# Two windowed attentions on one core: low parts on VectorE alone, a re-fitted layout clock, earlier release of key buffers, last outputs staged in pbuf

## The chip, the core and the metric

The kernel runs on one core of a Trainium2 chip. TensorE (PE) multiplies matrices, VectorE (DVE), ScalarE (ACT) and GpSimd (POOL) do the elementwise work, SyncE (SP) only issues DMAs. The metric is the device time of one launch in microseconds. Before the change three runs took 1970.92, 1972.98 and 1973.55 us; their median is 1972.98.

## What is computed

Two independent attention layers over 2048 positions with 1024 features and 32 heads of 32 features, all in fp32. Cut to what matters:

```
def A(x, wqkv, wo):               # sliding, dilated: 8 keys, every second position back
    q, k, v = split_heads(x @ wqkv)
    kg, vg = k[:, :, idx], v[:, :, idx]          # idx = pos - 2 * (0..7), masked below 0
    attn = softmax(einsum("bhsd,bhswd->bhsw", q, kg) * 32 ** -0.5)
    return concat_heads(einsum("bhsw,bhswd->bhsd", attn, vg)) @ wo

def B(x, wqkv, wo):               # sliding: the 256 positions up to its own
    q, k, v = split_heads(x @ wqkv)
    p = softmax(where(0 <= i - j < 256, q @ k.T * 32 ** -0.5, -1e9))
    return concat_heads(p @ v) @ wo

out = concatenate([A(...), B(...)], axis=-1)
```

## The kernel before

The work is cut into eight units of 512 positions: four of layer B ("dense" units, 0 to 3) and four of layer A ("window" units, 4 to 7, the even and the odd positions apart, so that the window is 8 neighbours). A unit has eight head groups of four heads. Each fp32 operand is split into a high part of reduced precision and a low part that holds the rest, and every large product is three matmuls: high by high, high by low, low by high (`TERMS`).

Weights and activations come from HBM as 512 KB tiles into three `raw` buffers (`Stream`). `parts` splits them: VectorE casts the high part (L129), and the low part, raw minus high, is made in halves of 512 columns by GpSimd (L134) or by VectorE (L137), whichever the planner expects to be done first, with a bias `POOL_BIAS`. After the first eight tiles GpSimd also issues the loads (L103).

A head group passes these stages. The query and key products (L363, 48 matmuls, t = 0 for queries and 1 for keys) end in a PSUM bank. ScalarE copies the high part out (L314), VectorE makes the low part (L318), and SyncE copies both into the stacked buffers `qst` and `kst` with three DMAs each (L328), after up to three reads of the halo, the keys of the unit before (L308). `qst` and `kst` are double buffered over the head groups, so the copies of head group hg wait for head group hg - 2; they stand in `waiting` until `finish` of that head group. The tiles of `natp`, from which they are copied, are two, so the eighth step of the next head group's product waits for these copies too.

Sixteen first products (L614) give the scores; VectorE finds the row maximum (L619), ScalarE the sum of the exponentials (L624), then its logarithm (L637). VectorE subtracts (L642) and splits the result (L644, L645), one small matmul, the row product (L653), turns it, VectorE copies it out (L657) and SyncE copies it into two further rows of `qst` (L660). The second products (L696 dense, L509 window) then give normalized exponents at once; ScalarE exponentiates them into `pbuf` (L701, L514), and masks are applied by VectorE (L685, L524) or GpSimd (L682, L520). Value products (L741, L548) follow, and `finish` copies their result out as high and low part (L577, L581). After a unit come the output products (L455) with `wo`, which are spread over the next unit's head groups (`O_SLOTS`), as value projections (L415) are over their own (`V_SLOTS`). Outputs go through one staging tile (`stp`, L379 or L382) and are stored by ScalarE's queue (L470).

All of this is put in order when the program is built. There are four lists of items, row products, second and values products, first products, and the large products. The class `Clock` holds the expected free time of each engine and of transfers; the loop at the end of the kernel takes at each step the item that is expected to be ready first. Every engine then runs its instructions in the order in which they were written, so the planner's costs (`C1`, `C3`, `CG`, `CV`, the durations given to `ck.use`, `ck.copy`, `ck.load`, `ck.fetch`) decide the order on every engine but nothing else.

For the last unit the output products of the first `TAIL` outputs run their first seven steps before the last head group is done; the eighth steps follow it.

## Time and profile before

| | before |
|---|---|
| median of three runs | 1972.98 us |
| profiled execution | 1973.82 us |
| its span, first to last instruction | 1972.1 us |
| mean granted TensorE clock | 0.987 |
| DMA | 294.92 MB, 150 GB/s over the span |

How to read it: busy times are per engine. A matmul's own duration overlaps with the next one's, so the rate of the matmuls is read from the chain of work that ended last, which gives stretches of them. "Idle before, releaser" in a group of instructions is the time that the engine stood still ahead of them and what ended it. PEclk is the clock that TensorE was granted; at half clock a matmul takes twice as long while TensorE counts as busy.

### The profile page before, as it was taken

What the parts mean: (1) busy time and instruction counts of PE and PEld (TensorE: products, weight loads), DVE (VectorE), ACT (ScalarE), POOL (GpSimd) and SP (SyncE); (2) the same over time, 40 slices, a digit from 0 to 9 for tenths busy, and PEclk for the clock granted to TensorE, in tenths of its full rate; (3) what the DMA queues carried; (4) which work ended last, traced back from release to release, by engine and by line L of the source; (5) the groups of instructions that cost most, each with busy time, mean ns of one, the idle gap of its engine ahead of it and who ended that gap; (6) DMA issues with size and microseconds to landing.
All of it is one profiled execution on the core that took longest, in us unless ns stands there. A gap on an engine that the chain in (4) does not pass through costs nothing.

```text
span 1972.1 us, 36479 instructions
## 1 busy us (share of the span) xinstructions
PE 1924.7 (98%) x12608; PEld 1619.8 (82%) x12608; DVE 1295.7 (66%) x3762; ACT 957.5 (49%) x3137; POOL 708.7 (36%) x923
## 2 busy tenths in 40 slices
PE   7999999999999999999999999999999999999998
PEld 6878887888877878788878888978888788888886
DVE  5687776678665786567865657655666557666653
ACT  3565554475654656555563344423534334434441
POOL 4334343444433434443443323233332333233221
PEclk9999999999999999999999999999989999999998
DMA  5555546455546465345645647455553565556442
GB/s 176 150 139 153 160 124 178 132 153 157 152 136 174 121 189 149 117 140 148 177 119 146 173 139 196 128 149 170 149 163 116 174 177 162 141 146 172 136 126 75
DMA packets 136502, 294.92 MB, mean 150 GB/s; under 512 B 14464, under 2 KB 42112, under 8 KB 136320
## 3 DMA queue, kind: packets, MB, share of 16 engines
q1 hardware_dynamic: 85632, 124.82, 26.1%
q0 software_dynamic: 40320, 146.82, 22.9%
q10 hardware_dynamic: 10368, 20.98, 2.9%
q8 instruction: 100, 1.64, 0.4%
q14 instruction: 82, 0.67, 0.1%
HBM read 163.58 MB, written 27.26 MB: 97 GB/s over the span
## 4 chain that ended last, share of the span: by engine, by line
PE 84%; DVE 7%; DMA 6%; ACT 2%; issue 1%; SPq 0%; POOL 0%; DVEq 0%; ACTq 0%; POOLq 0%
PE g L363 31%; PE g L455 16%; PE g L415 16%; PE s L614 7%; PE s L696 5%; PE o L741 4%; PE s L509 3%; DMA qst<-rt 3%; PE o L548 2%; DMA kst<-nat 1%; DMA raw<-xs 1%; DVE x L137 1%; DVE w L129 1%; ACT s L624 1%; DVE w L137 1%
## 5 line engine op out<-in xcount | busy, mean ns | idle before, releaser
L363 PE MATMUL g<-x,w 128*128 128x512 f32 x3072 | 801.9, 401 | 8.6 <-DVE w L129 8.0
L134 POOL TENSOR_TENSOR w<-raw,w 128x512 fp32r<-128x512 f32 x225 | 392.5, 1745 | 897.2 <-PE s L614 285.7
L363 PEld LDWEIGHTS g<-x,w 128*128 128x128 f32 x3072 | 562.0, 191 | 110.9 <-DVE w L129 8.4
L624 ACT ACTIVATE s<-s,nm 128x384 f32<-128x384 f32 (+3 forms) x1024 | 452.3, 443 | 231.0 <-DVE nm L619 227.1
L415 PE MATMUL g<-w,x 128*128 128x256 f32 x3072 | 413.3, 285 | 0.0
L415 PEld LDWEIGHTS g<-w,x 128*128 128x128 f32 x3072 | 392.7, 191 | 1.9 <-issue 0.6
L455 PE MATMUL g<-ot,w 128*128 128x512 f32 x1536 | 384.2, 397 | 3.6 <-DVE w L129 2.9
L455 PEld LDWEIGHTS g<-ot,w 128*128 128x128 f32 x1536 | 283.8, 190 | 58.1 <-DVE w L129 3.6
L619 DVE CUSTOM_DVE_ANT_0 s<-s,mask_d 128x384 f32<-128x384 f32 (+2 forms) x512 | 262.0, 556 | 72.9 <-PE s L614 71.5
L614 PE MATMUL s<-kst,qst 96*128 96x384 f32 (+3 forms) x1024 | 238.7, 303 | 16.2 <-ACT s L624 7.1
L701 ACT ACTIVATE pbuf<-s 128x384 f32<-128x384 f32 (+2 forms) x480 | 197.1, 507 | 85.5 <-PE s L696 81.8
L614 PEld LDWEIGHTS s<-kst,qst 96*128 96x128 f32 x1024 | 181.3, 192 | 60.5 <-ACT s L624 18.1
L624 ACT ACTIVATION_READ_ACCUMULATOR s<-s,nm 128x1 f32 x1024 | 210.2, 205 | 0.0
L619 DVE CUSTOM_DVE_ANT_0 s<-s,mask_w 128x136 f32<-128x136 f32 (+1 forms) x512 | 142.4, 322 | 98.4 <-PE s L614 96.8
L129 DVE CAST w<-raw 128x1024 fp32r<-128x1024 f32 x256 | 199.9, 781 | 9.4 <-PE g L455 9.4
L137 DVE TENSOR_TENSOR w<-raw,w 128x512 fp32r<-128x512 f32 x287 | 197.2, 696 | 8.8
L682 POOL TENSOR_SCALAR_AFFINE_SELECT pbuf<-pbuf 128x128 f32<-128x128 f32 (+1 forms) x383 | 147.9, 404 | 150.1 <-ACT pbuf L701 143.5
L314 ACT ACTIVATE nat<-g 128x512 fp32r<-128x512 f32 x128 | 76.6, 598 | 255.2 <-PE g L363 247.8
L318 DVE SCALAR_TENSOR_TENSOR nat<-g,nat 128x512 fp32r<-128x512 f32 x128 | 88.3, 690 | 145.5 <-ACT nat L314 134.9
L524 DVE TENSOR_TENSOR pbuf<-pbuf,keep_w 128x272 f32<-128x272 f32 (+1 forms) x224 | 116.9, 566 | 61.5 <-ACT pbuf L514 60.6
L619 DVE DVE_READ_ACCUMULATOR2_ANT nm<- 128x1 f32 x1024 | 144.3, 141 | 0.0
L696 PEld LDWEIGHTS s<-qst,kst 98*128 98x128 f32 x704 | 106.2, 189 | 37.8 <-PE o L741 10.0
(48 smaller groups left out, 1227.3 us busy)
## 6 DMA issues: line engine op xcount, KB each, us to landing
raw<-wqk POOLq DMA_DIRECT2D x126, 512.0 KB, 3.7
qst<-nat SPq DMA_DIRECT2D x192, 256.0 KB
kst<-nat SPq DMA_DIRECT2D x192, 256.0 KB
raw<-wo POOLq DMA_DIRECT2D x64, 512.0 KB, 3.7
raw<-wv POOLq DMA_DIRECT2D x62, 512.0 KB, 4.5
outs<-ost ACTq DMA_DIRECT2D x64, 256.0 KB
raw<-xs POOLq DMA_DIRECT2D x28, 512.0 KB, 4.8
halo<-nat SPq DMA_DIRECT2D x40, 256.0 KB
```

What stands on the lines that cost most here:

```text
L129: nc.vector.tensor_copy(t[:, 0, :], raw)
L134: nc.gpsimd.tensor_tensor(o, a, b, op=ALU.subtract)
L137: nc.vector.tensor_tensor(o, a, b, op=ALU.subtract)
L363: nc.tensor.matmul(h["ps"], h["w"][:, a, k * P:(k + 1) * P], xt[u][k][:, b, :], start=(k == 0 and i == 0), stop=(k == NK - 1 and i == 2))
L415: nc.tensor.matmul(ps, xt[u][k][:, a, p0:p0 + P], h["w"][:, c, k % kw], start=(k == 0 and i == 0 and r == 0), stop=(k == NK - 1 and i == 2 ...
L455: nc.tensor.matmul(h["ps"], h["w"][:, a, k * P:(k + 1) * P], ot[u, k][:, b, :], start=(k == 0 and i == 0), stop=(k == NK - 1 and i == 2))
L614: nc.tensor.matmul(ps[:, :n], q[0:96, j, b * P:(b + 1) * P], kk[0:96, j, c0:c1], start=True, stop=True)
L619: nc.vector.tensor_tensor_reduce(ps[:, :n], ps[:, :n], mask[:, cut:full], scale=-1.0, scalar=BIG, op0=ALU.add, op1=ALU.min, accum_out=nm)
L624: nc.scalar.activation(ps[:, :n], ps[:, :n], AF.Exp, bias=nm, scale=-1.0, accum_out=sm)
L682: nc.gpsimd.affine_select(w, w, pattern=[[0, m], [step, n]], compare_op=ALU.is_ge, fill=0.0, base=base, channel_multiplier=chan)
L696: nc.tensor.matmul(ps[:, i * n:(i + 1) * n], kk[0:98, j, 256 + kb * P:256 + (kb + 1) * P], q[0:98, j, q0:q0 + n], start=True, stop=True)
L701: nc.scalar.activation(w, ps[:, :pack * n].rearrange("p (j n) -> p j n", j=pack), AF.Exp)
```

## The change

Seven things are done together.

1. `POOL_BIAS` is -99, so every low part of loaded data is made by VectorE. GpSimd keeps masks and the issue of loads. In the masks that may go to either (`keep`) the bias is now `MASK_BIAS`, 0.2 as before, but the times that are compared have changed.
2. `Clock` is rewritten: it knows that some VectorE instructions (`port=True`) and GpSimd exclude each other, it gives every engine its own time from an instruction's end to its being seen, and every kind of transfer its own duration, on one shared list of busy stretches in place of two queues.
3. Costs are re-fitted throughout.
4. The high parts' copies into `qst` and `kst` are planned as soon as ScalarE is done; only the low part's copy follows VectorE. The halo reads move ahead of the query copies.
5. The copies that wait for head group hg - 2 are released 0.3 us after the issue of its last second product (`free_keys`), no longer at `finish`.
6. In the first unit the value projections go to slots 0, 2, 4, 7 (`V0_SLOTS`), no longer 0, 1, 5, 7.
7. In the last unit `TAIL` is 4 (the fourth output takes a PSUM bank of the score ring), outputs are staged in four slots of `pbuf`, and the weights of the last five output products are split as two tiles of 512 columns ("xw"), to be used one by one.

```diff
-POOL_BIAS = 0.6
+POOL_BIAS = -99
+MASK_BIAS = 0.2
+V0_SLOTS = {0:0,2:1,4:2,7:3}
-TAIL, LAND, XAT = 2, 0.45, 1
-C1, C3, CG, CV = 0.114, 0.2, 0.231, 0.243
+TAIL, XAT = 4, 1
+C1, C3, CG, CV = 0.108, 0.2, 0.231, 0.242
...
-    SEM = 0.17
+    SEM = 0.2
+    SEEN = dict(act=0.15, dve=0.115, pool=0.08)
+    LEAD = dict(sp=1.34, act=0.97, pool=1.43)
+    HOLD = dict(sp=0.63, act=0.35, pool=0.6)
+    MOVE = dict(load=(2.12, 0.14), store=(0.64, 0.4), copy=(1.18, 0.56), rows=(0.37, 0.56),
+                halo_out=(0.4, 0.68), halo_in=(0.55, 0.6), halo_few=(0.28, 0.51))
...
+    def start(self, eng, port, *ready):
+
+        t = max((self.free[eng],) + ready)
+        if eng == "pool":
+            t = max(t + 0.06, self.port["dve"])
+        elif port:
+            t = max(t, self.port["pool"])
+        return t
...
-            if max(ck.free["pool"], r) + 1.73 <= max(ck.free["dve"], r) + 0.62 + POOL_BIAS:
+            if ck.ends("pool", 1.15, r) <= ck.ends("dve", 0.61, r, port=True) + POOL_BIAS:
                 nc.gpsimd.tensor_tensor(o, a, b, op=ALU.subtract)
-                end = max(end, ck.use("pool", 1.73, r))
+                end = max(end, ck.use("pool", 1.15, r))
             else:
                 nc.vector.tensor_tensor(o, a, b, op=ALU.subtract)
-                end = max(end, ck.use("dve", 0.62, r))
+                end = max(end, ck.use("dve", 0.61, r, port=True))
...
-            item(p, "w", wo[ly, p[2]])
+            item(p, "w" if p[1] < U - 1 or p[2] < 3 else "xw", wo[ly, p[2]])
...
+            def place(part, e):
+                dst, c = (qst[buf], 0) if t == 0 else (kst[buf], 256)
+                for i, a in enumerate((0, 0, 1) if t == 0 else (0, 1, 0)):
+                    if a == part:
+                        nc.sync.dma_start(dst[i:96:3, :, c:c + S].bitcast(F32), hl[:, a, :].bitcast(F32))
+                        e2 = ck.copy("copy", e, ck.now)
+                return e2
+
+            def stack_hi():
+                if t == 0 and has_halo:
+                    read_halo()
+                h2["hi"] = place(0, r)
+
+            def later(f):
+                if hg < 2 or hg - 2 in done["second"]:
+                    f()
                 else:
-                    waiting.setdefault(hg - 2, []).append(stack)
+                    waiting.setdefault(hg - 2, []).append(f)
...
-                o = stp.tile([P, S], F32, tag="ost", name="ost")
-                e = copy_out(o, h["ps"], h["b"], rg)
+                o = pbuf[:, n % 4, :S] if last else stp.tile([P, S], F32, tag="ost", name="ost")
+                e = copy_out(o, h["ps"], h["b"], ring)
...
+            if ki == nk - 1 and hp == 4 // pack - 1:
+                free_keys(hg)
...
+    def free_keys(hg):
+
+        done["second"][hg] = ck.now
+
+        def go():
+            for f in waiting.pop(hg, []):
+                f()
+
+        ck.defer(ck.now + 0.3, go)
+
     def finish(u, s, h):
         hg = u * NG + s
         done["o"][hg] = ck.now
-        for f in waiting.pop(hg, []):
-            f()
...
         def keep(w, mask, n, m, step, base, chan, r):
-            dur_p, dur_d = m * n / 960 + 0.16, (m * n + 66) / 960
-            if max(ck.free["pool"], r) + dur_p <= max(ck.free["dve"], r) + dur_d + 0.2:
+            dur_p, dur_d = m * n / 960 + 0.13, m * n / 960 + 0.07
+            if ck.ends("pool", dur_p, r) <= ck.ends("dve", dur_d, r, port=True) + MASK_BIAS:
```

## The prediction

> **What bounds the kernel now.** I read the busy times first, then the granted clock, then the stages, then who made TensorE wait.
>
> ```profile
> span 1972.1 us, 36479 instructions
> ...
> PE 1924.7 (98%) x12608; PEld 1619.8 (82%) x12608; DVE 1295.7 (66%) x3762; ACT 957.5 (49%) x3137; POOL 708.7 (36%) x923
> ```
>
> ```profile
> core 0: 1972.1 us, clock 0.987
> ```
>
> TensorE sets the time. It is idle for 1972.1 - 1924.7 = 47.4 us and loses (1 - 0.987) x 1972 = 25.6 us to a halved clock. The change leaves its 12608 matmuls alone, so 73 us is all that any relayout can win. Six stages (start, first unit, its end, the other three dense units, four window units, tail) show where they lie:
>
> ```profile
> core 0: us, PE busy (x) PEld busy (x) DVE busy (x) ACT busy (x) POOL busy (x), PEclk, DMA share, GB/s
> 0.00:40.00 40.00, 29.35 (x152) 24.03 (x153) 22.33 (x48) 11.34 (x20) 17.64 (x28) 0.96 0.66 202
> 40.00:190.00 150.00, 147.97 (x910) 119.01 (x909) 109.35 (x344) 91.75 (x294) 58.42 (x78) 1.00 0.49 139
> 190.00:222.00 32.00, 29.60 (x183) 25.59 (x182) 28.84 (x80) 16.13 (x52) 11.41 (x15) 0.95 0.59 176
> 222.00:1040.00 818.00, 809.13 (x5302) 670.82 (x5302) 569.67 (x1530) 468.92 (x1357) 341.94 (x536) 1.00 0.52 148
> 1040.00:1900.00 860.00, 844.99 (x5710) 728.44 (x5708) 538.01 (x1691) 350.85 (x1357) 269.09 (x257) 0.99 0.55 156
> 1900.00:1972.00 72.00, 63.61 (x363) 51.86 (x361) 27.48 (x73) 18.50 (x60) 10.21 (x11) 0.88 0.19 66
> ```
>
> Idle is 10.7, 2.0, 2.4, 8.9, 15.0 and 8.4 us. The clock is lost in a few places, each row (1 - clock) x 50 us:
>
> ```profile
> 1200.00:1250.00 50.00, 48.20 (x347) 44.00 (x349) 37.34 (x115) 19.32 (x76) 13.80 (x16) 0.93 0.61 174
> ...
> 1450.00:1500.00 50.00, 47.52 (x351) 42.70 (x352) 27.97 (x94) 23.08 (x88) 15.08 (x15) 0.90 0.49 139
> ...
> 1650.00:1700.00 50.00, 47.62 (x334) 41.83 (x334) 39.37 (x122) 22.04 (x88) 14.39 (x15) 0.93 0.65 183
> ...
> 1900.00:1950.00 50.00, 45.08 (x282) 36.84 (x281) 26.10 (x71) 16.15 (x56) 8.43 (x10) 0.83 0.22 75
> ```
>
> That is 3.5, 5.0 and 3.5 us at the ends of three window units and 8.5 us in the tail: 20.5 of the 25.6. The waits of TensorE, by whom it waited for (total, times, longest):
>
> ```profile
> PE g L363 <- DVE w L129: 8.0, 1, 8.0
> PE s L614 <- ACT s L624: 7.1, 8, 1.2
> PE s L509 <- DMA qst<-rt: 6.7, 10, 1.8
> PE s L614 <- DMA kst<-nat: 5.7, 5, 2.0
> PE s L653 <- DVE hl L645: 3.4, 10, 0.5
> PE g L455 <- DVE w L129: 2.9, 1, 2.9
> PE s L696 <- DMA qst<-rt: 2.4, 4, 0.8
> ```
>
> The 8.0 us is the first load, which stays. Otherwise TensorE waits for the copy of the row sums into the query buffer (9.1), for key copies (5.7), for ScalarE at unit ends (7.1) and for the sums themselves (3.4). All are latencies that the order of work failed to cover, which is what this change re-plans.
>
> **Part 1, low parts by VectorE only.** The costs of the engines:
>
> ```profile
> L134 POOL TENSOR_TENSOR w<-raw,w 128x512 fp32r<-128x512 f32 x225 | 392.5, 1745 | 897.2 <-PE s L614 285.7 <-issue 243.3 <-DVE w L129 211.9
> ...
> L129 DVE CAST w<-raw 128x1024 fp32r<-128x1024 f32 x256 | 199.9, 781 | 9.4 <-PE g L455 9.4
> L137 DVE TENSOR_TENSOR w<-raw,w 128x512 fp32r<-128x512 f32 x287 | 197.2, 696 | 8.8
> ...
> L682 POOL TENSOR_SCALAR_AFFINE_SELECT pbuf<-pbuf 128x128 f32<-128x128 f32 x233 | 82.6, 375 | 74.7 <-ACT pbuf L701 72.9 <-DVE pbuf L685 0.3
> ...
> L685 DVE TENSOR_TENSOR pbuf<-pbuf,keep_f 128x128 f32<-128x128 f32 x183 | 53.9, 299 | 59.9 <-ACT pbuf L701 53.4
> ...
> L642 DVE TENSOR_TENSOR nl<-nm,ln 128x16 f32<-128x16 f32 x64 | 37.6, 588 | 15.1 <-ACT ln L637 14.9
> L685 DVE TENSOR_TENSOR pbuf<-pbuf,keep_d 128x128 f32<-128x128 f32 x96 | 37.3, 400 | 7.4 <-ACT pbuf L701 6.9 <-POOL pbuf L682 0.2
> ```
>
> GpSimd loses 225 x 1.745 = 392 us. VectorE gains 225 x 0.696 = 157 us. In the order of the new kernel's instructions, narrow masks go the other way: keep_f on VectorE 183 to 31, keep_d 96 to 38, so VectorE sheds 152 x 0.299 + 58 x 0.400 = 69 us, and GpSimd gets 210 more selects x 0.375 = 79 us. Wide masks move a little the same way, uncounted. VectorE would stand at 1296 + 157 - 69 = 1384 us (70%), GpSimd near 395 us (20%). But VectorE's present times hold waits for GpSimd. Minimum, median and maximum in ns of two of its groups, and one such meeting:
>
> ```profile
> L642 DVE TENSOR_TENSOR nl<-nm,ln x64: 165/176/1268, 48.3 to 1915.6; 128x16 f32<-128x16 f32 x64
> ```
>
> ```profile
> L129 DVE CAST w<-raw x256: 671/687/1791, 7.3 to 1952.2; 128x1024 fp32r<-128x1024 f32 x128
> ```
>
> ```profile
> 192.38 1.79 POOL L134 TENSOR_TENSOR w<-raw,w 128x512 fp32r<-128x512 f32 x1 [1.96 <-DVE w L129]
> ...
> 192.93 1.78 DVE L129 CAST w<-raw 128x1024 fp32r<-128x1024 f32 x1
> ```
>
> A cast of 0.69 us that starts 0.55 us into GpSimd's subtract takes 1.78. Mean against median, 256 x (0.781 - 0.687) + 64 x (0.588 - 0.176) = 24 + 26 = 50 us of such waits in two groups. With the long subtracts gone VectorE ends between 1334 and 1384 us, and the tiny subtract at L642, which stands in the chain to every row product, gets shorter by up to 0.4 us. [...] I take 0 us on TensorE for this part itself: in the list above TensorE waits for a low part almost nowhere between the start and the tail. If that cover went, in the end stage 190 to 222, where VectorE is already at 28.84 of 32 us, three moved subtracts cost 2 us there.
>
> **Part 2, the new planning clock.** It changes only the order. I added up the matmuls that stand between a producer and its consumer in each order, at rates from the chain:
>
> ```profile
> 1818.27 10.88 PE g L455 x48
> ...
> 1848.35 5.08 PE g L415 x42
> ```
>
> 0.227 us for 512 columns, 0.121 for 256. From the row product (L653) to the first second product, before: median 4.1 us, under 4 us at 28 of 64 heads; after: median 5.7, under 4 at 5. The copy itself takes, in the chain:
>
> ```profile
> 1413.89 3.27 DMA qst<-rt
> 1448.75 4.26 DMA qst<-rt
> ```
>
> With a VectorE copy ahead, 4 to 5 us are needed, which explains the 9.1 us and says that the wider cover takes most of it: -7 (bounds 0 and -9). From last first product to row product the cover goes from a median of 4.7 to 5.5 us, but falls to 0.3, 0.7, 0.7, 2.1 and 1.2 us at the last but one head of the four dense units and at the last head. Before, waits there were at most 0.5 us at covers near 4.1, so up to 4.6 us are needed: these five places can cost 4.3 + 3.9 + 3.9 + 2.5 + 3.4 = 18 us, while the 3.4 us at the other heads shrink: -2 (bounds 0 and -3). At the same unit ends the old order has most of its 7.1 us of waits for ScalarE, and waits overlap, so the net bounds at the five places are 0 and +18; I take +6, nearer the low end because the first products ahead are themselves spaced by ScalarE's pace, which the count leaves out.
>
> **Part 3, keys freed at the last second product, high parts first.** In the old order the copies wait until the values product is issued, by the same count 2.3 to 4 us of matmuls later at most heads. They now start that much earlier; SyncE still issues the same DMAs, with the halo reads moved ahead of the query copies and so in front of them, 3 issues. A row copy behind them on SyncE waits with them. The 5.7 us for keys should mostly go: -4 (bounds +2, if SyncE's queue pays it back, and -6).
>
> **Part 4, last outputs from pbuf, four outputs deep.** The old tail in the chain:
>
> ```profile
> 1929.69 2.01 DMA outs<-ost
> ...
> 1932.43 0.70 DVE w L129
> ...
> 1933.17 35.37 PE g L455 x144
> ```
>
> The second output waits for the single staging tile's store, the next weight's cast is queued behind that copy on VectorE, and TensorE waits 2.9 us for it. With four pbuf slots this wait goes, and 30 matmuls (6.8 us) stand behind the last values product as cover: -4 (bounds -1, -6). Start: a little less port blocking, 0.
>
> **Clock.** Lost clock follows bunched waits. With row, key and tail waits shorter I take back 5 us at the window unit ends and 4 in the tail, of 20.5, and add 2 at the dense unit ends: -7 (bounds +4, -18). [...]
>
> **Sum.** 0 - 7 - 2 + 6 - 4 - 4 - 7 = -18. The profiled execution took 1973.8 us outside a span of 1972.1, 0.8 above the median of the three runs, 1972.98. So 1973 - 18 = 1955 us.
>
> **Rivals.** (a) Slower: the dense unit ends decide. With the first unit having no output products to fill in, the eighth step of the next head's query product waits for a tile still being copied, while the row product in front of it in the order blocks TensorE. Five exposures at their full 18 us, one more copy time (3.3 us, as of the row copy) behind each of the first three, 4 us more of lost clock, against 7 + 2 + 4 + 4 won: 1973 + 32 - 17 = 1988. For it: the covers of 0.3 and 0.7 us; VectorE at 90% in 190 to 222. Against: waits overlap, and the old order lost only 2.4 us there. It decides from about 17 us of new loss at these ends. (b) Waits only move: each cover closed opens another, 1969 to 1977. For it: TensorE is 98% busy. Against: the covers grow at nearly all heads. (c) The re-plan works nearly everywhere: terms at their good ends, -9 - 3 - 6 - 6 - 18 and 0 for the unit ends, -42: 1931. For it: 50 us of VectorE's blocking leaves with the subtracts, and that shortens every chain. Against: new covers of under 1 us.
>
> **How the numbers follow.** Forecast (1940 to 1968) 0.56, (c) 0.14, (b) 0.11, (a) 0.19. A measurement here can tell 0.2%, 4 us. Faster takes the forecast, (c) and a little of (b): 0.72; same 0.08; slower 0.20. Eight in ten reach from 1931, all of (c)'s gain, to 1984, most of the way to (a); the forecast's own range is 1940 to 1968.
>
> **What would show it.** Right: the waits on the row copy fall from 9.1 us to under 3; the L642 subtract's mean from 588 to near 200 ns and the cast's from 781 to near 700; VectorE between 1334 and 1384 us; no wait of 2.9 us in the tail; clock at 0.990 or more. Wrong: TensorE waiting over 3 us at a row product at the dense unit ends, PEclk under 0.95 there, or a TensorE wait on loads that GpSimd issued late.

## The result and the profile after

| | before | after |
|---|---|---|
| median of the runs | 1971.87 us (6 runs, 1969.52 to 1973.55) | 1965.8 us (6 runs, 1962.62 to 1969.21) |
| ratio after to before, 95% interval | | 0.9966 [0.9951, 0.9982] |
| profiled execution | 1973.82 us | 1968.67 us |
| its span | 1972.1 us | 1966.7 us |

The kernel became 6 us faster, where the forecast was 18 us. The time lies in the upper end of the forecast's own range, 1940 to 1968 us, and beside the 1969 to 1977 us of rival (b), the waits that only move. The same program, measured once more in another group of runs, stood at 0.9987 [0.9972, 1.0003] of the kernel before, which would be 3 us, with an interval that reaches to none.

The span and the busy times of the changed kernel, from the head of its profile (share of the span, number of instructions):

```profile
span 1966.7 us, 35954 instructions
...
PE 1915.7 (97%) x12608; PEld 1618.3 (82%) x12608; DVE 1268.2 (64%) x3743; ACT 960.4 (49%) x3138; POOL 377.2 (19%) x946
```

The granted clock of its core:

```profile
core 0: 1966.7 us, clock 0.989
```

TensorE's idle time did not shrink, it grew: 1966.7 - 1915.7 = 51.0 us, against 47.4. The lost clock went from 25.6 to 0.011 x 1966.7 = 21.6 us. What is left of the 5.4 us between the two spans is 5 us less of busy time, which I could not put down to one place.

TensorE's waits, by whom it waited for (total, times, longest, in us):

```profile
PE s L719 <- DVE hl L711: 11.1, 5, 3.4
PE g L411 <- DVE w L163: 9.1, 4, 8.2
PE s L762 <- DMA qst<-rt: 8.7, 4, 2.4
PE s L680 <- DMA kst<-nat: 4.7, 3, 1.9
PE s L565 <- DMA qst<-rt: 4.7, 5, 1.5
PE s L680 <- ACT s L690: 3.1, 4, 1.0
PE s L565 <- ACT s L690: 1.1, 1, 1.1
```

The lines have new numbers: L719 is the row product (before L653), L762 and L565 are the second products (L696, L509), L680 the first products (L614), L411 the query and key products (L363), L690 ScalarE's sums (L624), L163 and L171 the cast and the low part of loaded data (L129, L137), L726 the row copy's DMA (L660). `hl` are the row sums, split into high and low part, and `rt` is the row product copied out of PSUM; "row copy" stands for both its copy out of PSUM and the 16 KB DMA that follows. Three things are to be seen. The row copies (`qst<-rt`), which were to fall from 9.1 us to under 3, took 8.7 + 4.7 = 13.4 us, in 9 waits where there had been 14. The row products became the largest entry, 11.1 us in 5 waits, where it had been 3.4 us in 10. The tail's wait for a weight is gone from the list.

The six stages, in the columns of the prediction (us from the start; length, then busy time and count of each engine, granted clock, DMA share, GB/s):

```profile
0.00:40.00 40.00, 31.72 (x173) 27.01 (x174) 23.25 (x49) 11.16 (x18) 7.41 (x24) 1.00 0.68 204
40.00:190.00 150.00, 141.79 (x839) 114.58 (x838) 92.87 (x290) 85.51 (x269) 35.85 (x101) 0.95 0.50 135
190.00:222.00 32.00, 27.32 (x187) 23.07 (x185) 22.32 (x65) 14.70 (x46) 8.93 (x20) 0.95 0.38 114
222.00:1040.00 818.00, 806.21 (x5225) 670.89 (x5226) 540.32 (x1436) 469.73 (x1356) 238.26 (x624) 0.99 0.52 149
1040.00:1900.00 860.00, 847.73 (x5826) 732.70 (x5826) 558.94 (x1823) 363.04 (x1397) 83.11 (x171) 1.00 0.55 158
1900.00:1972.00 72.00, 60.92 (x366) 50.08 (x364) 30.49 (x85) 16.30 (x57) 3.62 (x7) 0.93 0.19 67
```

The first unit paid for what the window units won: in 40 to 190 idle rose from 2.0 to 8.2 us and the clock fell from 1.00 to 0.95, while in 1040 to 1900 idle fell from 15.0 to 12.3 us and the clock rounds to 1.00. From the first query matmul of one unit to that of the next, the first unit takes 6.0 us more than before, the fourth 2.1 and the fifth, which holds the change from dense to window units, 9.1; the last three window units save 4.4, 7.2 and 5.1, and the tail, from the last matmul of a query or key product to the end, 5.3. That is the profiled execution; in the repeat of the same program the first unit took 4.1 us more, and the fifth 9.0.

Three of the 50 us windows, two of the first unit and the one that stood at 0.90 before:

```profile
100.00:150.00 50.00, 47.51 (x296) 39.85 (x298) 31.34 (x100) 27.86 (x87) 12.43 (x36) 0.93 0.50 134
150.00:200.00 50.00, 43.80 (x236) 33.16 (x228) 31.41 (x96) 26.85 (x87) 11.20 (x29) 0.90 0.46 120
...
1450.00:1500.00 50.00, 48.89 (x388) 43.77 (x387) 38.01 (x136) 26.28 (x108) 4.71 (x10) 1.00 0.52 154
```

The groups that part 1 touches (count, then busy us and mean ns of one, then idle before):

```profile
L163 DVE CAST w<-raw 128x1024 fp32r<-128x1024 f32 x251 | 173.7, 692 | 0.9 <-DMA raw<-wqk 0.9
L171 DVE TENSOR_TENSOR w<-raw,w 128x512 fp32r<-128x512 f32 x502 | 330.4, 700 | 8.7
L708 DVE TENSOR_TENSOR nl<-nm,ln 128x16 f32<-128x16 f32 x64 | 10.8, 169 | 12.2 <-ACT ln L703 11.8
L748 POOL TENSOR_SCALAR_AFFINE_SELECT pbuf<-pbuf 128x128 f32<-128x128 f32 x443 | 134.3, 335 | 133.4 <-ACT pbuf L769 133.1
```

The waits between VectorE and GpSimd ("port waits") went as worked out: the cast from a mean of 781 to 692 ns, the tiny subtract from 588 to 169. VectorE is at 1268.2 us, even under the 1334 us that was its lower bound: the masks of the window units held port waits too (192 of 128x272, 94.1 us with a mean of 535 ns before, 74.2 with 436 after; before, the 20 window masks on VectorE that ran beside a GpSimd subtract took a mean of 1.52 us, the other 204 one of 0.47), and the wide dense masks on VectorE, which the prediction left uncounted, went from 74 instructions and 44.6 us to 36 and 14.9 us. An engine became freer and its dependents waited longer, which is what the experiments had to explain.

### The profile page after: what moved, and what is told of

Same layout as the page of the kernel before. It is cut to its first block, busy times and chain, and to the rows that moved or that the text cites. A ratio compares the mean times of both kernels' runs of the same rounds, so it can differ in the third digit from the quotient of the medians.

```text
span 1966.7 us, 35954 instructions
## 1 busy us (share of the span) xinstructions
PE 1915.7 (97%) x12608; PEld 1618.3 (82%) x12608; DVE 1268.2 (64%) x3743; ACT 960.4 (49%) x3138; POOL 377.2 (19%) x946
## 3 DMA queue, kind: packets, MB, share of 16 engines
q0 software_dynamic: 40320, 146.82, 23.2%
## 5 line engine op out<-in xcount | busy, mean ns | idle before, releaser
L411 PE MATMUL g<-x,w 128*128 128x512 f32 x3072 | 803.1, 401 | 9.2 <-DVE w L163 9.1
L411 PEld LDWEIGHTS g<-x,w 128*128 128x128 f32 x3072 | 562.3, 191 | 112.4 <-DVE w L163 11.2
L690 ACT ACTIVATE s<-s,nm 128x384 f32<-128x384 f32 (+3 forms) x1024 | 452.5, 443 | 296.7 <-DVE nm L685 290.9
L509 PE MATMUL g<-ot,w 128*128 128x512 f32 x1416 | 360.0, 397 | 0.7 <-ACT ot L643 0.7
L171 DVE TENSOR_TENSOR w<-raw,w 128x512 fp32r<-128x512 f32 x502 | 330.4, 700 | 8.7
L509 PEld LDWEIGHTS g<-ot,w 128*128 128x128 f32 x1416 | 260.1, 190 | 49.8 <-ACT ot L643 1.2
L748 POOL TENSOR_SCALAR_AFFINE_SELECT pbuf<-pbuf 128x128 f32<-128x128 f32 (+1 forms) x631 | 218.8, 377 | 299.3 <-ACT pbuf L769 297.0
L680 PE MATMUL s<-kst,qst 96*128 96x384 f32 (+3 forms) x1024 | 234.6, 302 | 9.5 <-DMA kst<-nat 4.7
L680 PEld LDWEIGHTS s<-kst,qst 96*128 96x128 f32 x1024 | 178.6, 190 | 50.6 <-issue 14.5
L685 DVE CUSTOM_DVE_ANT_0 s<-s,mask_w 128x136 f32<-128x136 f32 (+1 forms) x512 | 141.8, 322 | 112.7 <-PE s L680 112.1
L690 ACT ACTIVATION_READ_ACCUMULATOR s<-s,nm 128x1 f32 x1024 | 210.2, 205 | 0.0
L137 POOL DMA_DIRECT2D raw<-wqk x126 | 68.8, 546 | 589.4 <-DVE w L171 203.3
L163 DVE CAST w<-raw 128x1024 fp32r<-128x1024 f32 x251 | 173.7, 692 | 0.9 <-DMA raw<-wqk 0.9
L762 PEld LDWEIGHTS s<-qst,kst 98*128 98x128 f32 x704 | 110.1, 191 | 42.7 <-ACT s L690 15.7
L762 PE MATMUL s<-qst,kst 98*128 98x256 f32 (+2 forms) x704 | 135.3, 305 | 9.0 <-DMA qst<-rt 8.7
```

The lines of the kernel that those rows point to most:

```text
L163: nc.vector.tensor_copy(t[:, 0, :], raw)
L171: nc.vector.tensor_tensor(o, a, b, op=ALU.subtract)
L411: nc.tensor.matmul(h["ps"], h["w"][:, a, k * P:(k + 1) * P], xt[u][k][:, b, :], start=(k == 0 and i == 0), stop=(k == NK - 1 and i == 2))
L509: nc.tensor.matmul(h["ps"], w[:, a, c:c + P], ot[u, k][:, b, :], start=(k == 0 and i == 0), stop=(k == NK - 1 and i == 2))
L680: nc.tensor.matmul(ps[:, :n], q[0:96, j, b * P:(b + 1) * P], kk[0:96, j, c0:c1], start=True, stop=True)
L685: nc.vector.tensor_tensor_reduce(ps[:, :n], ps[:, :n], mask[:, cut:full], scale=-1.0, scalar=BIG, op0=ALU.add, op1=ALU.min, accum_out=nm)
```

## The experiments

Parts are numbered as in the prediction. The 15 runs went in four groups, each with its own runs of the kernel before: medians 1972.06 us (the first four), 1967.07 (the next four), 1971.99 (the next four) and 1974.7 (the last three). Ratios are to these; they are taken over all runs of a group and differ a little from the quotient of the medians. "Meetings" counts, in the trace, the row copies at whose issue a 512 KB load is issued within -0.3 to +0.8 us; there are 64 row copies. Before there are 5 meetings, in the changed kernel 19.

The theory came out of one place in the trace. The timeline of the changed kernel in its first unit (start us, duration, engine, line, operation, tiles; in brackets the idle time before it and what ended it):

```profile
160.63 0.17 DVE L711 TENSOR_TENSOR hl<-nl,hl 128x16 fp32r<-128x16 f32 x1
160.72 0.69 DVE L163 CAST w<-raw 128x1024 fp32r<-128x1024 f32 x1
...
161.44 1.29 DVE L171 TENSOR_TENSOR w<-raw,w 128x512 fp32r<-128x512 f32 x2
161.49 0.22 PE L719 MATMUL s<-ident,hl 128*32 128x128 f32 x1
...
162.65 0.27 DVE L723 CAST rt<-s 32x128 fp32r<-32x128 f32 x1
...
162.95 0.66 SPq L726 DMA_DIRECT2D qst<-rt  x1
163.04 0.53 POOL L137 DMA_DIRECT2D raw<-wv  x1 [5.15 <-DVE rt L723]
...
167.45 0.98 PE L762 MATMUL s<-qst,kst 98*128 98x384 f32 x2 [2.22 <-DMA qst<-rt]
```

Around the row product VectorE makes a whole split (cast and both halves, 160.72 to 162.73, 2.0 us) that the plan put ahead of the row copy. That delays the copy to 162.65, and the end of the split frees a raw buffer, so that GpSimd issues a 512 KB load 0.09 us after SyncE has issued the 16 KB row copy. The bracket at the load names the row copy, as the last signal before the issue, but the issue follows the end of the split by 0.30 us, and 226 of the 272 later loads of this run do so too; the same 0.30 us stand in the run below in which the row copy isn't made on VectorE. By the DMA packets of the trace this copy's first packet starts 3.1 us after its issue and its last ends after 3.82 us; a row copy of the same unit that met no load (136.27 us) has 1.3 and 1.74 us. Over all 64, the 19 that met a load have a median of 3.7 us. In the new order the loads are issued when VectorE has split, and VectorE's next work is often the row copy.

### Old order, low parts by VectorE

```diff
-                nc.gpsimd.tensor_tensor(o, a, b, op=ALU.subtract)
+                nc.vector.tensor_tensor(o, a, b, op=ALU.subtract)
```

> The old kernel with the old order on every engine but one: the 225 low parts that GpSimd made are now issued on VectorE, and the planner still believes that GpSimd makes them. Theory (the order decides; the engine only frees VectorE of waits): VectorE's casts fall from 781 to about 700 ns and the small subtract before the row product from 588 to below 200, TensorE's wait for row products and row copies shrinks by 2 to 4 us, 1967 to 1971 us against 1972. Rival (the engine change alone is the whole gain): 1963 to 1966, and the new order is worth nothing. Second rival (VectorE is too full at the unit ends): 1976 or more.

Measured: 2009.09 us, ratio 1.0193 [1.0166, 1.022]. That is far above the theory and the first rival. The second rival's "1976 or more" holds the number, but not its place: the new waits are for row copies and lie inside the units as well as at their ends. Two of TensorE's waits in it:

```profile
PE s L696 <- DMA qst<-rt: 14.8, 11, 2.5
PE s L509 <- DMA qst<-rt: 14.5, 15, 2.1
```

What follows: part 1 alone is not free. Without a plan that knows of it, the row copies' waits go from 9.1 to 29.3 us, with 20 meetings, while TensorE's order is the old one throughout. The forecast's "0 us on TensorE for this part itself" was looked up at the waits for low parts, and it is the row copy that pays.

### New order, every second half back on GpSimd

```diff
-                nc.vector.tensor_tensor(o, a, b, op=ALU.subtract)
+                (nc.gpsimd if c else nc.vector).tensor_tensor(o, a, b, op=ALU.subtract)
```

> The changed kernel with its own order, but the second 512 columns of each weight's low part (251 of 502) are issued on GpSimd, unknown to the planner. Theory: the new order's covers hold only while VectorE is not held up; casts go back to about 780 ns, masks on GpSimd queue behind 1.7 us subtracts, so 1972 to 1985 us. Rival (order alone is what won): 1964 to 1968, no change against the changed kernel.

Measured: 1962.22 us, ratio 0.995 [0.9932, 0.9968], below both ranges, with one meeting in 64. Of the row copies' waits 0.2 us are left, but the row products wait 16.3 us in 16 places and ScalarE's sums cost 7.7. So the new order can live with GpSimd's subtracts, and the row copies' waits hang on when the loads are issued, not on the cover in matmuls, which is the same here as in the changed kernel. What is won there is given back at the row products, whose tiny subtract (L708) is back at a mean of 676 ns, against 169 in the changed kernel.

### The old slots of the first unit

```diff
-V0_SLOTS = {0:0,2:1,4:2,7:3}
+V0_SLOTS = V_SLOTS
```

> The changed kernel with the value projections of the first unit in the old slots (0, 1, 5, 7). In the changed kernel the first unit got 6 us longer, 10 us without its faster start. Theory (the first unit has no output products to fill with, so any order of the new clock waits there): the first unit stays 3 to 10 us longer than in the old kernel, total 1962 to 1972 us. Rival (the new slots delay the values of heads 2 to 5 and so hold up the pbuf and the keys): the first unit returns to about 196 us, total 1957 to 1961 us.

Measured: 1964.0 us, ratio 0.996 [0.9945, 0.9975]. Its interval overlaps the changed kernel's almost wholly. The first unit returned to 197.0 us (195.6 before, 201.6 in the changed kernel), as the rival said, but the time didn't: the slots move waits, and nothing in the time that can be measured.

### Early key release in the old order

```diff
+            if ki == nk - 1 and hp == 4 // pack - 1:
+                free_keys(hg)
...
-        for f in waiting.pop(hg, []):
-            f()
```

(with the high parts' copies ahead, as in the change; the planner's clock is the old one)

> The old kernel with part 3 alone: high parts copied first, halo reads ahead of the query copies, keys released at the last second product; old clock, GpSimd low parts, old tail. Theory (copies start 2.3 to 4 us earlier, waits for keys of 5.7 us shrink): -2 to -6 us, 1966 to 1970. Rival (SyncE's queue pays it back: row copies stand behind copies that wait for VectorE, and the old clock does not know it): waits for row copies grow above 9 us and it comes out at 1974 to 1985.

Measured: 2030.63 us, ratio 1.0298 [1.0271, 1.0325], outside both ranges above, and the slowest run of all. Its largest wait:

```profile
PE s L637 <- DMA kst<-nat: 39.8, 22, 4.1
```

Waits for keys went from 5.7 to 39.8 us, while row copies took 6.6 us. In the old plan the part that was to shorten the waits for keys lengthens them. A plan that still believes in the old durations of a copy may put the first products too early; that is argued, not shown, as no run separates it.

### Loads held back

A GpSimd write of the raw tile in front of each load that GpSimd issues, so that the load comes later while the row copy stays on VectorE:

```diff
+            if not early:
+                self.nc.gpsimd.memset(raw, 0.0)
```

> The changed kernel with its order and engines, but GpSimd clears the raw buffer (128x1024) before it issues each later load, so that the load leaves about 1.4 us after VectorE's last subtract instead of 0.4. Theory (with both halves on VectorE the load of 512 KB is issued in the same tenths of a microsecond as the row copy that VectorE makes right after the subtract; 19 of 64 row copies meet one and take 3.7 us instead of about 2): under 8 of 64 row copies meet a load, TensorE's waits for row copies fall from 13.4 to under 8 us, 1957 to 1962 us. Rival (row copies are late because VectorE makes the split first): the waits stay above 11 us and the time at 1964 to 1970. Second rival (later loads or the clearing hold VectorE up): above 1970.

Measured: 1961.13 us, ratio 0.9971 [0.9956, 0.9985], one meeting; the changed program itself had 1964.87 in the same group. The row copies' waits fall from 13.4 to 0.9 us, with the order of TensorE, VectorE and ScalarE untouched. TensorE's first entry in this kernel, and the two of the row copies:

```profile
PE s L721 <- DVE hl L713: 20.0, 21, 3.4
...
PE s L764 <- DMA qst<-rt: 0.6, 3, 0.2
...
PE s L567 <- DMA qst<-rt: 0.3, 1, 0.3
```

The writes have a cost of their own: VectorE is busy for 1305.0 us, against 1268.2, the small cast ahead of the row product takes a mean of 551 ns, against 175, and the row products wait 8.9 us more. For the row copies the run is plain. On the 19 copies that met a load in the changed kernel, the time from row product to issue stays (medians of 1.45 us there and 1.46 here), as the split still stands ahead of the copy; the time from issue to landing falls from 3.7 to 1.8 us. So the waits follow the loads' moment of issue, and the rival, that the copies are late because VectorE makes the split first, is ruled out.

### Keys released at finish in the new plan

```diff
-        ck.defer(ck.now + 0.3, go)
+        release[hg] = go
...
-        done["o"][hg] = ck.now
+        done["o"][hg] = done["second"][hg] = ck.now
+        release.pop(hg)()
```

> The changed kernel planned with the keys released at the values product, as before, instead of at the last second product; high parts still go first. Theory (early release is worth about 2.5 us per head group where TensorE has nothing else, mostly in the first unit and at the dense unit ends): 1972 to 1985 us. Rival (the new clock is the gain, the early release is covered anyway): 1963 to 1968.

Measured: 1983.24 us, ratio 1.009 [1.006, 1.0119]; the changed program itself had 0.9987 in the same group (below). So the early release is worth about 20 us inside the new plan, while part 3 costs 59 us inside the old one: its price cannot be given without the plan around it.

### The old kernel with the new tail

```diff
-TAIL, LAND, XAT = 2, 0.45, 1
+TAIL, LAND, XAT = 3, 0.45, 1
...
-                o = stp.tile([P, S], F32, tag="ost", name="ost")
+                o = pbuf[:, n % 4, :S] if last else stp.tile([P, S], F32, tag="ost", name="ost")
```

(with the "xw" tiles of the last output products)

> The old kernel with part 4 alone (outputs of the last unit in four pbuf slots, the last weights in halves), three outputs deep because the fourth needs the new order. Theory: the 2.9 us wait in the tail goes and the halved clock there shrinks, -4 to -6 us, 1966 to 1968. Rival (the wait only moves behind the last row copy): 1970 to 1973.

Measured: 1961.47 us, ratio 0.9964 [0.9948, 0.998]. That is as much as the whole change gains, from one of its parts. Every engine's order is the old one up to the last unit, and that unit takes 288.8 us from its first query matmul, against 296.6 before.

The run also shows how far a list of waits moves by itself: with the same order ahead of the last unit its row copies waited 4.2 us, where the kernel before has 9.1.

### GpSimd in the new plan at its measured price

```diff
-POOL_BIAS = -99
+POOL_BIAS = 0.6
...
-            if ck.ends("pool", 1.15, r) <= ck.ends("dve", 0.61, r, port=True) + POOL_BIAS:
+            if ck.ends("pool", 1.75, r) <= ck.ends("dve", 0.61, r, port=True) + POOL_BIAS:
```

> The changed kernel re-planned with GpSimd allowed for low parts, at its measured 1.75 us and the old bias of 0.6. Theory (VectorE alone is a loss under the new clock, since it lines loads up with row copies): 1955 to 1962 us, the first unit near 196 us instead of 202. Rival (e2 won by chance of its order): 1963 to 1970.

Here the edit did nothing: at that price the plan gives every low part to VectorE, and the program is instruction for instruction the changed one. As a test of GpSimd it is void; as a repeat it gives 1964.87 us, 0.9987 [0.9972, 1.0003], which shows how far two groups can differ (0.9966 in the result above). Its row copies waited 11.9 us, where the list above has 13.4.

### The row copy on ScalarE

```diff
-                nc.vector.tensor_copy(rt, ps[0:32, 0:P])
-                e = ck.use("dve", 0.2, ck.now)
+                nc.scalar.copy(rt, ps[0:32, 0:P])
+                e = ck.use("act", 0.2, ck.now)
```

> The changed kernel with the copy of the row product out of PSUM on ScalarE instead of VectorE, planned so. Theory (a split of 1.9 us that VectorE starts while it waits for the row product stands in front of the row copy and frees the raw buffer at the same moment): the row copy no longer follows the subtract, fewer than 8 of 64 meet a load, TensorE's waits for row copies fall from 13 to under 8 us, and the time is 3 to 7 us under the changed kernel's 1965, 0.993 to 0.996 of the old kernel. Rival (ScalarE's queue holds the copy as long): waits of 10 us or more and no gain over 0.9966.

Measured: 1950.78 us, ratio 0.989 [0.987, 0.991], 4 meetings. Its waits at the row products and for row copies:

```profile
PE s L719 <- DVE hl L711: 13.0, 5, 3.4
...
PE s L565 <- DMA qst<-rt: 1.0, 1, 1.0
```

The time is below the 0.993 to 0.996 expected. The row copies' 13.4 us became 1.0, and nothing else in the list grew by more than 2 us. But the plan was made anew with this edit, which left one doubt for the last group.

### The changed kernel with the old tail

```diff
-TAIL, XAT = 4, 1
+TAIL, XAT = 2, 1
...
-                o = pbuf[:, n % 4, :S] if last else stp.tile([P, S], F32, tag="ost", name="ost")
+                o = stp.tile([P, S], F32, tag="ost", name="ost")
```

(with whole weight tiles to the end)

> The changed kernel with part 4 undone: two outputs ahead, one staging tile, last weights whole. Theory (part 4 is the whole net gain; new clock, early keys and VectorE together come out near zero): 0.998 to 1.003 of the old kernel, 1968 to 1976 us. Rival (the parts overlap, each would give the gain): 0.994 to 0.998, as the changed kernel.

Measured: 1972.02 us, ratio 0.9999 [0.9983, 1.0015]. The tail's wait is back, one line of its list:

```profile
PE g L509 <- DVE w L163: 3.4, 1, 3.4
```

TensorE's order is the changed kernel's up to the last unit, which takes 289.5 us, against 286.2. With the run on the old kernel this says where the net gain is: parts 1 to 3 with the new plan come to about nothing. The interval alone would give -3 to +3 us; as one program differed by 0.0021 between two groups, 4 us either way is what can be said.

### The row copy on ScalarE elsewhere

The same edit on the old kernel with the new tail:

```diff
-                nc.vector.tensor_copy(rt, ps[0:32, 0:P])
+                nc.scalar.copy(rt, ps[0:32, 0:P])
```

> The old kernel with part 4 (three outputs deep) and the row copy on ScalarE. Theory (in the old order only 5 of 64 row copies meet a load and VectorE's split with one half is shorter, so the copy's engine matters less): within 3 us of the old kernel with part 4 alone, 0.994 to 0.998 of the old kernel. Rival (VectorE's queue is what makes row copies late in both orders): 0.990 to 0.993.

Measured: 1965.28 us, ratio 0.9964 [0.9948, 0.998], the same ratio as without it. And together with GpSimd's halves:

```diff
-                nc.vector.tensor_tensor(o, a, b, op=ALU.subtract)
+                (nc.gpsimd if c else nc.vector).tensor_tensor(o, a, b, op=ALU.subtract)
...
-                nc.vector.tensor_copy(rt, ps[0:32, 0:P])
+                nc.scalar.copy(rt, ps[0:32, 0:P])
```

> The changed kernel with both: second halves of the weights' low parts on GpSimd, unknown to the planner, and the row copy on ScalarE. Theory (both remove the same meeting, so the gains do not add): 0.992 to 0.996 of the old kernel. Rival (they are separate losses): under 0.992.

Measured: 1974.4 us, ratio 1.0007 [0.9992, 1.0022], above both ranges. In these runs the move of the row copy helped where row copies meet loads (19 times in the changed kernel) and brought no gain where they don't (5 times before, once with GpSimd's halves). Why the last of these is slower than GpSimd's halves alone is open: its row products wait 17.7 us and ScalarE's sums 8.9, in a plan made anew.

### The row copy on ScalarE in the same order

The copy is made on ScalarE, and the plan still books it on VectorE, so that TensorE's instructions stand exactly as in the changed kernel:

```diff
-                nc.vector.tensor_copy(rt, ps[0:32, 0:P])
+                nc.scalar.copy(rt, ps[0:32, 0:P])
                 e = ck.use("dve", 0.2, ck.now)
```

> The row copy is made on ScalarE, but the plan still books it on VectorE, so that TensorE's instructions stand in exactly the order of the changed kernel. Theory (the row copy stood behind a 1.9 us split on VectorE and its 16 KB copy was issued together with the 512 KB load which that split frees; the move of engine parts them): TensorE's waits for row copies fall from 13.4 us to under 4 us with this order too, few of the 64 row copies meet a load (under 8, against 19), and the time is 1950 to 1957 us. Rival (the gain came from the new plan, which put other matmuls between a row copy and the second products): the waits for row copies stay above 9 us and the time is 1963 to 1968 us.

Measured: 1946.81 us, ratio 0.9856 [0.9839, 0.9872], clock 0.992, 5 meetings. The theory's waits and meetings hold: no row copy is left in the list of waits. The time is below the 1950 to 1957 us expected. The timeline of the same head, which comes 7.5 us earlier because the heads before it lost less:

```profile
153.94 1.29 DVE L171 TENSOR_TENSOR w<-raw,w 128x512 fp32r<-128x512 f32 x2
153.98 0.22 PE L719 MATMUL s<-ident,hl 128*32 128x128 f32 x1
154.24 0.26 ACT L723 CAST rt<-s 32x128 fp32r<-32x128 f32 x1 [2.05 <-PE s L719]
154.52 0.66 SPq L726 DMA_DIRECT2D qst<-rt  x1
...
155.53 0.53 POOL L137 DMA_DIRECT2D raw<-wv  x1 [5.12 <-DVE nm L685]
...
157.67 0.52 PE L762 MATMUL s<-qst,kst 98*128 98x384 f32 x2
```

From the row product to the row copy's issue it is 0.54 us, where it was 1.46; the load comes 1.01 us behind it, where it was 0.09; by the packets the copy lands in 1.74 us, where it took 3.82; and the second product has no wait in front of it. So the gain doesn't need a new plan. This edit takes away both the delay behind the split and the meeting with the load; the run with held-back loads, in which the delay stayed and the waits went all the same, says that the meeting is what TensorE waited for.

### A third tile of natural-layout products

The other large wait of the changed kernel, at the row product near a dense unit's end, in the same view:

```profile
476.04 0.86 PE L411 MATMUL g<-x,w 128*128 128x512 f32 x3
...
478.82 0.22 ACT L703 ACTIVATE ln<-sm 128x16 f32<-128x16 f32 x1
...
479.81 0.22 PE L719 MATMUL s<-ident,hl 128*32 128x128 f32 x1 [2.91 <-DVE hl L711]
479.87 0.91 PE L411 MATMUL g<-x,w 128*128 128x512 f32 x3
```

The last three matmuls of the next query product stand behind the row product, since their tile of `natp` is still being copied when the order needs work. The kernel with the row copy on ScalarE therefore got a third tile, and room for it by nine x tiles:

```diff
-NX, NST = 10, 1
+NX, NST = 9, 1
...
-    natp = ctx.enter_context(tc.tile_pool(name="natp", bufs=2))
+    natp = ctx.enter_context(tc.tile_pool(name="natp", bufs=3))
...
-                if k == NK - 1 and hg:
-                    return done["nat"].get((hg - 1, t)) and max(xready[u][k], done["nat"][hg - 1, t] - 0.6)
+                old = (hg - 1, 0) if t else (hg - 2, 1)
+                if k == NK - 1 and old[0] >= 0:
+                    return done["nat"].get(old) and max(xready[u][k], done["nat"][old] - 0.6)
```

> As the kernel with the row copy on ScalarE, with three tiles of natural-layout products instead of two, nine x tiles instead of ten to make room for them, and the last eighth of a product allowed one product earlier. Theory (at the ends of the dense units the row products wait because the next query product can't take its last step before the tile's stack copies are done, so that little work is left to put between): TensorE's waits at the row products fall from 13.0 us to under 6 us and the time is 1938 to 1946 us, if nine x tiles cost nothing by the control. Rival (nothing of the tiles is at fault, the order has no other work there): the waits at the row products stay at 11 us or more, and the time is that of the control within 4 us.

The control has nine x tiles and the row copy on ScalarE, nothing else:

> Control for the run with three tiles: the row copy on ScalarE and nine x tiles, nothing else. Both theories: 1950 to 1956 us, as with ten x tiles, since the loads of x are issued many us ahead; if the ninth tile matters, the wait shows at the matmuls that read w behind the split on VectorE.

Measured: 1936.89 us with three tiles, ratio 0.981 [0.9795, 0.9825], and 1947.24 us for the control, 0.986 [0.9845, 0.9875]. Waits at the row products and for row copies, three tiles:

```profile
PE s L720 <- DVE hl L712: 3.7, 4, 2.3
...
PE s L566 <- DMA qst<-rt: 0.9, 1, 0.9
```

and the control:

```profile
PE s L719 <- DVE hl L711: 14.1, 6, 3.6
```

Both times are a little below their ranges. 14.1 us became 3.7, a difference of 10.4, and so is that of the two medians; that the two agree so well is partly chance, as waits for ScalarE grew from 6.2 to 10.0 us and the granted clock rose from 0.992 to 0.996. The control runs the order of the kernel with ten x tiles on every engine, so its 0.986 beside that kernel's 0.989 is again the difference of two groups. The place above then looks like this, in the third tile's timeline:

```profile
456.71 1.55 PE L412 MATMUL g<-x,w 128*128 128x512 f32 x6
458.73 1.93 PE L412 MATMUL g<-x,w 128*128 128x512 f32 x6 [0.47 <-DVE w L163]
...
461.25 0.22 PE L720 MATMUL s<-ident,hl 128*32 128x128 f32 x1 [0.60 <-DVE hl L712]
```

Twelve matmuls of the query and key products stand where there were three. This version, 1936.89 us, is the best of the study, below both kernels.

## Why the prediction was right in direction and wrong in size

- **Row copies, -7 forecast, +4.3 measured (9.1 to 13.4 us): the step that failed.** The prediction counted matmuls between the row product and the second products and took 4 to 5 us as what is needed, "with a VectorE copy ahead", as a fixed sum. The cover (those matmuls) did grow, but so did the need: the split on VectorE stands ahead of the copy and frees a load onto the DMA engines at the same moment. On the 19 copies that met a load, row product to issue has a median of 1.45 us and issue to landing one of 3.7, 5.2 us together; on the other 45 it is 0.57 and 2.3. Part 1 was costed at 0 us because no TensorE wait names a low part; the price was in VectorE's queue and at the raw buffer that it frees. Delaying the loads alone, or moving the copy off VectorE alone, removed these waits with TensorE's order unchanged. The error of 11.3 us in this term is the largest. With 3.0 us each for keys and clock and about 1 for the tail the errors are more than the 12 us by which the sum was off; the 5 us less of busy time, which no term held and no run explains, went the other way.
- **Row products and unit ends, -2 + 6 = +4 forecast: right.** The four last-but-one heads of the dense units waited 3.4, 2.9, 2.9 and 0.6 us (9.9 in 222 to 1040). With the first of them, and a clock of 0.93 in 200 to 250, two of the prediction's signs of being wrong came, without rival (a) deciding. Waits at row products rose from 4.9 to 12.1 us, for hl and for ScalarE together, those of the first and second products for ScalarE fell from 7.1 to 4.2: +4.3 net. The mechanism named under rival (a), the eighth step behind a tile still being copied, is what the third tile confirmed, at 10.4 us and far from the 17 us at which it would decide. One reading was short: "at most 0.5 us" of earlier waits there leaves out two that the list puts down to ScalarE, of which the longer was 0.9.
- **Early keys, -4 forecast, -1.0 in the list (5.7 to 4.7 us).** The size was off, and the runs say that the term has no price by itself: the early release gains about 20 us in the new plan, and part 3 loses 59 us in the old.
- **Tail, -4 and 4 us of clock there: right in place.** The 2.9 us wait is gone, the tail is 5.3 us shorter, its window 1900 to 1950 went from 0.83 to 0.93. Alone on the old kernel the part won 7 us by the ratio, 5.6 by the medians.
- **Clock, -7 forecast, -4.0 measured.** The window units' ends recovered all of their 12 us, more than the 5 forecast. The first unit lost as much anew, in the windows from 100 to 250 (0.93, 0.90 and 0.93), where the row copies now wait, and near 224 us a row product. With the row copy on ScalarE in the same order the three windows stand at 1.00, 0.97 and 0.97. So most of this error is the first one again.
- **VectorE's port waits: right,** and of no use to TensorE, as VectorE's busy time was not what bound. VectorE fell 66 us below its lower bound, 50 of them by the window masks' shorter times (20 us) and the wide masks that moved (30 us), neither of which the prediction counted.

Rival (b) described the outcome of parts 1 to 3 (0.9999 with the old tail), for another reason than the one given: at the row copies the cover held, and the latency behind it grew. That the total came near nothing doesn't make each part small: the early release moves it by about 20 us, and the row copies' meetings with loads by about 19 (1965.8 to 1946.81).

## What to carry to other kernels

Before counting the cover in front of a small, urgent transfer, look at what stands ahead of its producer on that engine and what the end of that work sets free: a buffer's release can be the issue of a load, whose packets then go ahead of the small transfer's (here from 164.28 us against 166.06, though the load was issued 0.09 us after the copy). Try such a copy on an engine that doesn't free large loads, and check the pairs of issue times in the trace first: where few pairs met, 5 of 64 before, the move brought nothing here, 0.9964 with it and without, on the old kernel with the new tail. A cost that no wait names can still be paid by another instruction in the same queue: part 1 was forecast at 0 us, and the waits for row copies stood at 13.4 us.

## What the runs showed of the hardware

A 16 KB copy that was issued within 0.1 us of a 512 KB load from another queue started to move about 1.8 us later than one of the same unit that met none (first packet after 3.1 us, against 1.3); the medians are 3.0 us for the 19 copies that met a load and 1.8 for the other 45. In the place shown above the load's packets run from 164.28 to 166.47 us, and the first of the copy's stands at 166.06. The queue of the loads in the changed kernel (packets, MB, share of 16 engines):

```profile
q0 software_dynamic: 40320, 146.82, 23.2%
```

With 280 loads (126 + 64 + 62 + 28 by the page's DMA issues), a load takes, by my estimate from this line, about 0.232 x 1966.7 / 280 = 1.6 us on each of the 16 DMA engines, in 40320 / 280 / 16 = 9 packets, if it is spread evenly over them. So the copy lost about as much as one load's whole share takes. In what order an engine takes the packets of two queues was not shown.

The clock fell to 0.90 and 0.93 in windows where no wait of TensorE listed was over 2.4 us (100 to 200 in the changed kernel), and back to 1.00 and 0.97 when these waits left with the row copy on ScalarE in the same order. In 40 to 190 the waits came to 6.2 us more of idle time and about 0.05 x 150 = 7.5 us of clock. That is no fixed price: in 1040 to 1900 of the same run, 12.3 us of idle time stand beside a clock that rounds to 1.00. In the clock records of the two kernels' traces the clock is halved in stretches of 3.41 us or two, three or five times that, but for the last, which the end of the run cuts off: in the changed kernel for 6.83 us from 112.7, in the wait of 2.44 us that ends at 113.25, and for 3.41 us from 167.3, in that of 2.22 us that ends at 167.45, but not at the wait of 1.45 us that ends at 1532.63. In the kernel before, TensorE stood idle for 1.4 to 2.8 us of the 5 us ahead of each of the seven stretches that begin within its span; 1.6 us of idle time within 5 us, near 470, 730 and 1545 us, brought none. In the seven the matmuls of its query and key products (L363) follow each other every 427 ns, against 231 outside them, and take 628 ns each, against 392 (medians): not quite twice.
